# RWKV attention and a gated feed-forward on one core: channel loads of the filled rows only

## The chip, the core and the metric

The kernel runs on one core of a Trainium2 chip. The metric is the device time of one execution in microseconds (us). One core has a TensorE (PE, matmuls; its weight loads are shown as PEld), a VectorE (DVE), a ScalarE (ACT), a GpSimd (POOL), a SyncE (SP) that issues nearly all of this kernel's transfers, and 16 DMA engines that carry them out.

## What is computed

A linear attention with a decaying state (4 batches, 8 heads, 768 tokens, 48 channels per head) feeds a gated feed-forward with 3072 tokens, width 384 and inner width 1536. Cut to what matters:

```python
for t in range(S):
    kt, vt, rt = k[:, :, t], v[:, :, t], r[:, :, t]
    cur = einsum('bhd,bhe->bhde', u[None] * kt, vt)
    y[:, :, t] = einsum('bhd,bhde->bhe', rt, state + cur)
    state = w[None, :, :, None] * state + einsum('bhd,bhe->bhde', kt, vt)
x = y.transpose(0, 2, 1, 3).reshape(B * S, H * D)
out = (sigmoid(x @ w_gate) * (x @ w_val)) @ w_out
```

## The kernel before

The attention is worked off in chunks of 64 tokens (12 of them), each split into two groups of heads: 24 groups, numbered n. A group's r and k come by channels in a tile `chan` (128 partitions x 2 x 512 floats, 4 KB per partition) and its k and v by tokens in a tile `toks`. A head has 48 channels, and two heads lie in one tile, so partitions 0 to 47 and 64 to 111 of `chan` hold data and partitions 48 to 63 and 112 to 127 hold zeros, which the host wrote into the input. `load_channels` (line 97) takes a buffer out of a pool of three and loads all 128 rows with one transfer of 512 KB (line 100).

A `chan` tile is read by `bonus_keys` (ACT, L273, the first eight groups), `queries` (L294, on POOL or DVE), `keys` (DVE, L300, which multiplies the k half in place) and `scores` (PE, L341), which reads the rows 0 to 47 and 64 to 111 alone. `apply` (PE, L313) makes the attention output, `x_high` and `x_low` (L449, L453) write it into the tile `xt` of the feed-forward, and `fills` moves the channels of one pair of heads to their rows inside `xt` with small transfers of 16 rows (`fill`, L457). The feed-forward of a tile of two chunks is twelve slices f: `up` (PE, L495) reads `xt`, and `down` (PE, L533) sums into three accumulators. Its weights come as 64-bit words, are loaded once in the first part (`load_weights`, L223) and turned into two parts by DVE, ACT and POOL.

The order on every engine is the program's order. The first eight groups and the first tile are written out by hand in a string `START`; in it `L.n` is `load_channels(n)`, `X.n` `load_tokens(n)`, `W.f` `load_weights(f)`, `F.n` `fills(n)`. Its channel loads come in the order 0, 1, 2, 3, 4, 7, 5, 6. A loop over slices then does the other sixteen groups and loads each of them about two groups ahead. SP issues its transfers in this order as well. Its transfers use eight semaphores in turn (DMAHW0 to DMAHW7 in the listings below), and each transfer waits until the one eight places before it has landed, so no more than eight are under way.

Of the kernel before, what the change touches and what calls it, by code (L numbers as in the profile page):

```python
# [9 lines left out]
F32 = mybir.dt.float32  # L10
# [7 lines left out]
B, H, S, D = 4, 8, 768, 48  # L18
DM, DF = H * D, 1536
P = 128  # L20
# [37 lines left out]
def rwkv_then_moe(ctx: ExitStack, tc: tile.TileContext, wd, ch, tk, rt, ut, wt, rk0, vn0, wd0, out):  # L58
    nc = tc.nc
# [7 lines left out]
    ring = ctx.enter_context(tc.tile_pool(name="ring", bufs=3, space=PSUM))  # L67
    pacc = ctx.enter_context(tc.tile_pool(name="pacc", bufs=1, space=PSUM))
    main = ctx.enter_context(ExitStack())
    ach = main.enter_context(tc.tile_pool(name="ach", bufs=3))  # L70
    atk = main.enter_context(tc.tile_pool(name="atk", bufs=3))
    adk = main.enter_context(tc.tile_pool(name="adk", bufs=2))
    xp = main.enter_context(tc.tile_pool(name="xp", bufs=2))
# [2 lines left out]
    def two_banks():  # L76
        return ps.tile([P, 2, 512], F32, name="sc")
# [14 lines left out]
    nc.sync.dma_start(out=wu, in_=wd)  # L92
    w = wu[:, 0]

    chan, toks = {}, {}

    def load_channels(n):
        c, g = GROUPS[n]
        chan[n] = ach.tile([P, 2, 512], F32, name="chan")
        nc.sync.dma_start(out=chan[n], in_=ch[c, g])  # L100

    def load_tokens(n):
        c, g = GROUPS[n]
# [229 lines left out]
    def scores(n):  # L333
        t, r, k = dec[n], chan[n][:, 0], chan[n][:, 1]
        sc = ga[n] = two_banks()
        for kk, rr, at in ((k, t[:, 0], 0), (t[:, 1], r, 256))[: 1 if n >= FIRST else 2]:
            for p, p2 in PP:
                o = at + (2 * p + p2) * C
                for be, gm in QUARTERS:
                    row, cs = slice(64 * be, 64 * be + D), (4 * p + 2 * (be ^ gm) + p2) * C  # L340
                    nc.tensor.matmul(  # L341
                        sc[64 * gm : 64 * gm + 64, be ^ gm, o : o + C],
                        kk[row, cs : cs + C], rr[row, cs : cs + C], start=True, stop=True,
                    )

    def keep(n):
        sc, t = ga.pop(n), score[n % 2]
        if n >= FIRST:
            nc.vector.copy_predicated(
                t.rearrange("q (m i) -> q m i", m=8),  # L350
                masks[:, 1].bitcast(I32).unsqueeze(1).broadcast_to([P, 8, C]),
                gains[n % 2].unsqueeze(2).broadcast_to([P, 8, C]),
            )
        for m, at in ((0, 0), (1, 256))[: 1 if n >= FIRST else 2]:
            nc.vector.copy_predicated(  # L355
                t.rearrange("q (b m i) -> q b m i", b=2, m=4),
                masks[:, m].bitcast(I32).unsqueeze(1).unsqueeze(1).broadcast_to([P, 2, 4, C]),
                sc[:, :, at : at + 256].rearrange("q b (m i) -> q b m i", m=4),
            )

    def apply(n):
        c, g = GROUPS[n]
        v, t = toks[n][:, 1], score[n % 2]
        yb[n] = one_bank(), one_bank()
        if c:
            from_state(n)
            if n < FIRST or n + 1 == len(GROUPS):
                nc.tensor.drain()
            else:
                scores(n + 1)  # L370
                if GROUPS[n][0] < NC - 1:
                    outer(n, ga[n + 1][:, :, 256:512])
                for b in range(2):
                    nc.vector.tensor_copy(seen[:, b : b + 1], yb[n][b][0:112, 0:1])
        for p, p2 in PP:
            for s in range(2):
                for gm in range(2):
                    be, row = gm ^ s, slice(64 * gm, 64 * gm + 64)
                    m, at = D if s else 64, (4 * p + 2 * s + p2) * D
                    i = (4 * s + 2 * p + p2) * C  # L380
                    into_y(
                        n, s, be, m, slice((2 * p + p2) * C, (2 * p + p2 + 1) * C),
                        v[row, at : at + m], t[row, i : i + C], True,
                    )
# [203 lines left out]
    def finish(i):  # L588
# [8 lines left out]

    steps = {
        "L": load_channels, "X": load_tokens, "W": load_weights, "A": bonus_keys, "R": queries,
        "k": keys, "T": token_keys, "Z": scores, "K": keep, "I": apply, "O": outer,  # L600
        "d": decay_state, "s": add_state, "h": x_high, "l": x_low, "F": fills, "D": finish,
        "tc": constants, "tk": channel_table, "ti": inverses, "tp": token_powers,
# [15 lines left out]
    for step in START.split():  # L618
        name, _, arg = step.partition(".")
# [12 lines left out]
    def load(n):  # L632
        load_channels(n)
        load_tokens(n)

    n = FIRST
# [5 lines left out]
    for i in range(n0, len(items)):  # L642
        ti, h, f = items[i]
# [4 lines left out]
        if i == n0 + 2:  # L648
            gain(n)
            scores(n)  # L650
            keep(n)
            load(n + 2)
# [35 lines left out]
    with tc.If(bad != 0):  # L688
        with ExitStack() as g:
# [22 lines left out]
            with tc.For_i(0, NC) as c:  # L712
                for p in range(NP):
                    nc.sync.dma_start(
                        out=rkc[:, p].rearrange("q a b i -> q (a b i)"),
                        in_=rk0[bass.ds(c, 1), p].rearrange("o q x -> (o q) x"),
                    )
                with tc.For_i(0, C) as i:
                    for lo, side in ((0, 1), (64, 0)):
# [3 lines left out]
                        for p in range(NP):  # L723
                            nc.sync.dma_start(
                                out=vb[lo : lo + D, p], in_=src[:, p].broadcast_to([D, B, 64])
# [25 lines left out]
                    out=xg[bass.ds(c, 1)].rearrange("o q p t -> (o q) p t"),  # L751
                    in_=yc.rearrange("q p b i -> q p (b i)"),
# [3 lines left out]
            with tc.For_i(0, NC, 2) as c:  # L756
                for j in range(3):
                    for to, lo, n, p in (
# [3 lines left out]
                            out=xr[to : to + n, j],  # L762
                            in_=xg[bass.ds(c, 2), lo : lo + n, p].rearrange("c q t -> q c t"),
# [108 lines left out]
```

## Time and profile before

| | us |
|---|---|
| median of 3 runs | 541.75 (540.87 to 541.93) |
| profiled execution | 540.73 |
| its span | 538.94 |
| PE busy in the span | 518.4 (96%) |
| DVE busy | 216.4 (40%) |
| DMA traffic of SP's queue | 46.81 MB, 25.4% of the span of 16 engines |
| `chan` loads | 24 of 512 KB, median 4.9 from issue to landing |

The profiled execution is read by stretches: the share of busy time over the whole span hides that PE waits only in the first 110 us, where the transfers are dense too. "Landing" is the moment at which the last of a transfer's 16 engines has reported; a row of the transfers in a window gives the time from the start of the issue to it.

### The profile page before, as it was taken

How to read it: one execution, taken by the hardware profiler on the slowest of the kernel's cores; microseconds unless marked ns; L12 is line 12 of the kernel's file. 1: busy time of each engine (PE TensorE's matmuls, PEld its weight loads, DVE VectorE, ACT ScalarE, POOL GpSimd, SP SyncE). 2: the span in 40 equal slices, each digit the busy share in tenths (PEclk: the TensorE clock that was granted, in tenths of full speed). 3: DMA queues.
4: the chain of work that ended last, by engine and by line, in shares of the span. 5: the costliest groups of instructions: out<-in, count | busy, mean ns of one | idle time of the engine just before them, and what ended most of it. 6: DMA issues, size and time to landing. Idle time of an engine off the chain costs nothing.

```text
span 538.9 us, 12058 instructions
## 1 busy us (share of the span) xinstructions
PE 518.4 (96%) x5268; PEld 425.6 (79%) x5268; DVE 216.4 (40%) x375; ACT 171.3 (32%) x354; POOL 174.8 (32%) x159
## 2 busy tenths in 40 slices
PE   2889999999999999999999999999999999999996
PEld 2778878788788887888888888888888887888885
DVE  7999989912343342432413414313414311111111
ACT  5485755522132322231332222312322212221121
POOL 3424022122814444244145144143242311111120
PEclk9999999999999999999999999999999999999998
DMA  8895705053022214220303402203400001100001
GB/s 318 312 338 217 286 1 186 15 205 128 2 86 86 66 50 144 85 74 12 95 3 103 145 5 82 65 30 106 144 1 16 11 2 19 60 1 1 0 1 63
DMA packets 15706, 48.03 MB, mean 89 GB/s; under 512 B 2368, under 2 KB 5056, under 8 KB 14240
## 3 DMA queue, kind: packets, MB, share of 16 engines
q1 hardware_dynamic: 15360, 46.81, 25.4%
q8 instruction: 43, 0.70, 0.5%
q10 hardware_dynamic: 288, 0.39, 0.2%
q14 instruction: 15, 0.12, 0.1%
HBM read 40.12 MB, written 4.72 MB: 83 GB/s over the span
## 4 chain that ended last, share of the span: by engine, by line
PE 91%; DMA 4%; DVE 1%; SPq 1%; issue 1%; ACT 0%; POOL 0%; DVEq 0%; ACTq 0%; POOLq 0%
PE ring L495 56%; PE acc L533 27%; PE ring L313 5%; PE sc L341 2%; DMA xt<-xt 1%; DMA chan<-in_ch 1%; PE sc L396 1%; DMA wr<-in_wt 1%; SPq L457 1%; PE sc L533 1%; POOL dec L294 0%; DVE wf L236 0%; DVE wx L246 0%; ACT wx L243 0%; ACT wf L229 0%
## 5 line engine op out<-in xcount | busy, mean ns | idle before, releaser
L495 PE MATMUL ring<-xt,wx 128*128 128x512 f32 (+1 forms) x1332 | 316.4, 391 | 1.4 <-DMA xt<-xt 1.2
L495 PEld LDWEIGHTS ring<-xt,wx 128*128 128x128 f32 x1332 | 246.1, 190 | 56.6 <-issue 1.3
L517 POOL TENSOR_TENSOR h<-sg,h 128x512 fp32r<-128x512 f32 (+1 forms) x68 | 86.7, 1276 | 298.8 <-ACT h L513 298.8
L533 PE MATMUL acc<-h,wx 128*128 128x512 f32 (+1 forms) x666 | 161.1, 383 | 0.0
L508 DVE TENSOR_TENSOR sg<-ring,sg 128x512 f32<-128x512 f32 (+1 forms) x74 | 49.9, 676 | 275.6 <-PE ring L495 275.6
L533 PEld LDWEIGHTS acc<-h,wx 128*128 128x128 f32 x666 | 119.6, 188 | 24.4
L504 ACT ACTIVATE sg<-ring 128x512 f32<-128x512 f32 (+1 forms) x74 | 43.4, 587 | 184.3 <-PE ring L495 181.2
L513 ACT CAST h<-sg 128x512 fp32r<-128x512 f32 (+1 forms) x74 | 45.3, 613 | 112.0 <-DVE sg L508 111.1
L415 ACT ACTIVATE state<-state,every 112x96 f32<-112x96 f32 x80 | 23.5, 365 | 26.2 <-PE ring L313 26.2
L294 POOL TENSOR_TENSOR dec<-chan,every 128x512 f32<-128x512 f32 x21 | 25.9, 1233 | 17.0 <-DMA chan<-in_ch 12.7
L453 DVE TENSOR_TENSOR xt<-ring,xt 112x256 fp32r<-112x256 f32 (+1 forms) x52 | 20.0, 419 | 24.9 <-ACT xt L449 24.4
L341 PE MATMUL sc<-dec,chan 48*64 48x64 f32 x768 | 17.4, 231 | 7.9 <-DVE dec L294 7.9
L355 DVE COPY_PREDICATED score<-masks,sc 128x512 f32<-128x512 int32 x32 | 23.9, 745 | 1.5 <-PE sc L341 0.6
L449 ACT CAST xt<-ring 112x256 fp32r<-112x256 f32 (+1 forms) x52 | 17.1, 373 | 19.6 <-PE ring L313 17.0
L341 PEld LDWEIGHTS sc<-dec,chan 48*64 48x64 f32 x768 | 15.0, 145 | 9.3 <-DVE dec L294 7.9
L313 PE MATMUL ring<-score,toks 64*48 64x64 f32 (+1 forms) x768 | 18.7, 230 | 3.7 <-POOL dec L294 1.6
L304 POOL TENSOR_TENSOR toks<-toks,tabn 128x384 f32<-128x384 f32 x20 | 21.1, 1059 | 1.7 <-ACT tabn L194 1.6
L313 PEld LDWEIGHTS ring<-score,toks 64*48 64x48 f32 (+1 forms) x768 | 15.3, 133 | 5.1 <-POOL dec L294 1.8
L313 PEld LDWEIGHTS ring<-dec,state 48*48 48x48 f32 (+1 forms) x704 | 12.4, 127 | 8.3 <-issue 7.4
L300 DVE TENSOR_TENSOR chan<-chan,every 128x512 f32<-128x512 f32 x24 | 17.2, 715 | 0.9 <-ACT dec L273 0.9
L246 POOL TENSOR_TENSOR wx<-wf,wx 128x1152 fp32r<-128x1152 f32 (+1 forms) x3 | 6.8, 2262 | 31.9 <-ACT wx L243 31.9
L282 POOL TENSOR_TENSOR dec<-dec,toks 128x384 f32<-128x384 f32 x16 | 16.3, 1017 | 1.2
(61 smaller groups left out, 260.0 us busy)
## 6 DMA issues: line engine op xcount, KB each, us to landing
wr<-in_wt SPq DMA_DIRECT2D x11, 1152.0 KB, 8.0
chan<-in_ch SPq DMA_DIRECT2D x24, 512.0 KB, 4.9
toks<-in_tk SPq DMA_DIRECT2D x24, 400.0 KB, 5.0
out_y<-wf SPq DMA_DIRECT2D x16, 256.0 KB, 2.3
dec<-in_rt SPq DMA_DIRECT2D x16, 192.0 KB, 2.6
xt<-xt SPq DMA_DIRECT2D x30, 64.0 KB, 2.3
wr<-in_wt SPq DMA_DIRECT2D x2, 576.0 KB, 5.4
xt<-xt SPq DMA_DIRECT2D x12, 32.0 KB, 5.1
```

The lines of the kernel that those rows point to most:

```text
L294: eng.tensor_tensor(v4(t[:, 0]), v4(chan[n][:, 0]), bc2(table_of(n)), ALU.mult)
L304: eng.tensor_tensor(v4(k), v4(k), bc2(tabn[:, 4 * g : 4 * g + 4]), ALU.mult)
L313: nc.tensor.matmul(yb[n][bank][64 * half : 64 * half + m, cs], lhsT, rhs, start=first, stop=stop, skip_group_check=True,)
L341: nc.tensor.matmul(sc[64 * gm : 64 * gm + 64, be ^ gm, o : o + C], kk[row, cs : cs + C], rr[row, cs : cs + C], start=True, stop=True,)
L355: nc.vector.copy_predicated(t.rearrange("q (b m i) -> q b m i", b=2, m=4), masks[:, m].bitcast(I32).unsqueeze(1).unsqueeze(1).broadcast_to ...
L415: nc.scalar.activation(st[:, p, s], st[:, p, s], AF.Copy, scale=pw[0:112, 4 * g + 2 * p + s, 64:65],)
L495: nc.tensor.matmul(o[:, self.cols], w[a][:, g * DM + kt * P : g * DM + (kt + 1) * P], self.x[:, kt, b, self.cols], start=(k == 0), stop=(k ...
L504: nc.scalar.activation(sg[:, c], self.pair[f][0][:, c], AF.Sigmoid)
L508: nc.vector.tensor_tensor(sg[:, c], self.pair.pop(f)[1][:, c], sg[:, c], ALU.mult)
L513: nc.scalar.copy(out=h[:, 0, c], in_=sg[:, c])
L517: eng.tensor_tensor(h[:, 1, c], self.sg.pop(f)[:, c], h[:, 0, c], ALU.subtract)
L533: nc.tensor.matmul(acc[:, to], w[a][:, 2 * DM + d * P : 2 * DM + (d + 1) * P], h[:, b, cols], start=(f == 0 and k == 0 and self.cols.start ...
```

## The change

`chan` is no longer a rotating pool of three buffers but three named tiles, held in a list. The first load into each still takes all 128 rows. Every later load (21 of 24) is two transfers of 48 rows, 192 KB each; the zero rows stay from the first load (`keys` multiplies them in place, and zero stays zero). A buffer goes back to the list when the `scores` of its group have been written down in the program.

```diff
-    ach = main.enter_context(tc.tile_pool(name="ach", bufs=3))
+    ach = main.enter_context(tc.tile_pool(name="ach", bufs=1))
...
+    CHANNELS = slice(0, D), slice(64, 64 + D)
     chan, toks = {}, {}
+    cbuf = [ach.tile([P, 2, 512], F32, name=f"chan{i}") for i in range(3)]
 
     def load_channels(n):
         c, g = GROUPS[n]
-        chan[n] = ach.tile([P, 2, 512], F32, name="chan")
-        nc.sync.dma_start(out=chan[n], in_=ch[c, g])
+        whole = len(chan) < 3
+        chan[n] = cbuf.pop(0)
+        for rows in (slice(0, P),) if whole else CHANNELS:
+            nc.sync.dma_start(out=chan[n][rows], in_=ch[c, g, rows])
...
     # at the end of scores(n)
+        cbuf.append(chan[n])
```

On SP, before, from the weights of slice 2 on (`wr`): two channel loads (groups 7 and 5) stand ahead of the six small fills of `xt` for group 2.

```order
L223 DMA wr<-in_wt 128x1152 [waits DMAHW3_49]
L105 DMA toks<-in_tk 128x800 [waits DMAHW4_49,PE_49,Pool_49]
L223 DMA wr<-in_wt 128x1152 [waits DMAHW5_49]
L223 DMA wr<-in_wt 128x1152 [waits DMAHW6_49]
L105 DMA toks<-in_tk 128x800 [waits DMAHW7_49,PE_49,Pool_49]
L100 DMA chan<-in_ch 128x1024 [waits DMAHW0_49]
L100 DMA chan<-in_ch 128x1024 [waits DVE_49,DMAHW1_49,PE_49,Activation_49]
L457 DMA xt<-xt 16x2x256 [waits DMAHW2_49,DVE_49]
L457 DMA xt<-xt 16x2x256 [waits DMAHW3_49]
L457 DMA xt<-xt 16x2x256 [waits DMAHW4_49]
L457 DMA xt<-xt 16x2x256 [waits DMAHW5_49]
L457 DMA xt<-xt 16x2x256 [waits DMAHW6_49]
```

The sixth fill of this batch (not in the piece) waits on DMAHW7, which the `toks` load shown in the fifth row uses. On SP in the same place now, from that `toks` load on:

```order
L109 DMA toks<-in_tk 128x800 [waits DMAHW1_49,PE_49,Pool_49]
L104 DMA chan_97<-in_ch 48x1024 [waits DMAHW2_49]
L104 DMA chan_97<-in_ch 48x1024 [waits DMAHW3_49]
L104 DMA chan_95<-in_ch 48x1024 [waits DVE_49,DMAHW4_49,PE_49,Activation_49]
L104 DMA chan_95<-in_ch 48x1024 [waits DMAHW5_49,PE_49]
L462 DMA xt<-xt 16x2x256 [waits DMAHW6_49,DVE_49]
L462 DMA xt<-xt 16x2x256 [waits DMAHW7_49]
L462 DMA xt<-xt 16x2x256 [waits DMAHW0_49]
L462 DMA xt<-xt 16x2x256 [waits DMAHW1_49]
L462 DMA xt<-xt 16x2x256 [waits DMAHW2_49]
L462 DMA xt<-xt 16x2x256 [waits DMAHW3_49]
```

Two issues more stand ahead of the fills, and the semaphores have moved: the last three fills wait for the `toks` load and for the two halves of group 7's load, where before they waited for the two `wr` loads and the `toks` load.

On PE, in the loop, the first sixteen products of one `scores`; before:

```order
L341 MATMUL sc<-dec,chan 64x64 [waits DMAHW5_49,Pool_49]
L341 MATMUL sc<-dec,chan 64x64 x15
```

and now:

```order
L345 MATMUL sc<-dec,chan_97 64x64 [waits DMAHW7_49,Pool_49]
L345 MATMUL sc<-dec,chan_97 64x64
L345 MATMUL sc<-dec,chan_97 64x64 [waits DMAHW0_49]
L345 MATMUL sc<-dec,chan_97 64x64 x13
```

The third product, the first that reads the rows 64 to 111, has a wait of its own for the second half. DVE's `keys` and POOL's `queries` now wait for two transfers in one place.

## Rows read from the trace of the kernel before

**Rows 1.** The page: busy time, share of the span, instructions of each engine.
```profile
PE 518.4 (96%) x5268; PEld 425.6 (79%) x5268; DVE 216.4 (40%) x375; ACT 171.3 (32%) x354; POOL 174.8 (32%) x159
```

**Rows 2.** Stretches: us, length, PE, PEld, DVE, ACT, POOL busy (instructions), clock, DMA share, GB/s.
```profile
31.00:39.00 8.00, 6.39 (x184) 5.51 (x182) 7.86 (x14) 5.76 (x16) 1.94 (x3) 1.00 0.88 320
39.00:50.00 11.00, 10.21 (x212) 9.49 (x213) 10.83 (x17) 6.09 (x16) 6.72 (x7) 1.00 0.52 183
50.00:110.00 60.00, 59.38 (x643) 47.68 (x642) 54.53 (x67) 35.68 (x59) 9.97 (x6) 1.00 0.38 136
110.00:430.00 320.00, 320.00 (x3160) 260.17 (x3159) 100.62 (x209) 84.13 (x186) 125.27 (x109) 1.00 0.22 72
```

**Rows 3.** The chain that ended last, 29 to 45 us: start, us, what.
```profile
31.56 0.09 SPq L457
31.65 0.04 issue
31.69 7.41 DMA xt<-xt
39.10 0.14 issue
39.24 2.53 PE ring L495 x18
```

**Rows 4.** Instructions by time on PE: start, us, what [idle before <- releaser].
```profile
22.01 1.08 PE L313 MATMUL ring<-toks 64*64 64x48 f32 x30 [0.38 <-DVE xt L453]
...
23.02 4.21 PE L495 MATMUL ring<-xt,wx 128*128 128x256 f32 x18
...
39.24 2.53 PE L495 MATMUL ring<-xt,wx 128*128 128x256 f32 x18 [1.18 <-DMA xt<-xt]
```

**Rows 5.** SP's issues by time, 3 to 36 us: start, us, what.
```profile
3.09 1.22 SPq L100 DMA_DIRECT2D chan<-in_ch  x2
4.36 0.98 SPq L105 DMA_DIRECT2D toks<-in_tk  x2
9.98 0.33 SPq L100 DMA_DIRECT2D chan<-in_ch  x1
...
15.28 0.33 SPq L100 DMA_DIRECT2D chan<-in_ch  x1
16.16 0.33 SPq L105 DMA_DIRECT2D toks<-in_tk  x1
16.54 4.59 SPq L457 DMA_DIRECT2D xt<-xt  x6
21.17 0.58 SPq L223 DMA_DIRECT2D wr<-in_wt  x1
...
29.32 0.33 SPq L105 DMA_DIRECT2D toks<-in_tk  x1
29.70 0.92 SPq L100 DMA_DIRECT2D chan<-in_ch  x2
31.05 4.95 SPq L457 DMA_DIRECT2D xt<-xt  x6
...
34.59 1.42 SPq L457 DMA_DIRECT2D xt<-xt  x2
```

**Rows 6.** Transfers in windows that hold one issue: count, KB, us to landing.
```profile
chan<-in_ch SPq DMA_DIRECT2D x1, 512.0 KB, 7.2
...
chan<-in_ch SPq DMA_DIRECT2D x1, 512.0 KB, 7.7
...
toks<-in_tk SPq DMA_DIRECT2D x1, 400.0 KB, 8.8
...
chan<-in_ch SPq DMA_DIRECT2D x1, 512.0 KB, 6.4
...
chan<-in_ch SPq DMA_DIRECT2D x1, 512.0 KB, 5.5
...
xt<-xt SPq DMA_DIRECT2D x1, 32.0 KB, 2.5
...
toks<-in_tk SPq DMA_DIRECT2D x1, 400.0 KB, 6.1
...
chan<-in_ch SPq DMA_DIRECT2D x1, 512.0 KB, 8.4
...
xt<-xt SPq DMA_DIRECT2D x1, 32.0 KB, 4.5
```

**Rows 7.** Stretches, columns as in rows 2: whole loads; last landings; fills alone.
```profile
5.00:13.00 8.00, 3.47 (x120) 3.31 (x124) 6.82 (x12) 5.33 (x15) 1.46 (x1) 1.00 1.02 412
19.40:22.90 3.50, 1.82 (x51) 1.51 (x44) 3.38 (x8) 2.21 (x4) 2.14 (x2) 1.00 0.52 110
...
82.47:82.97 0.50, 0.50 (x4) 0.41 (x3) 0.50 (x2) 0.43 (x2) 0.00 (x0) 1.00 0.76 123
```

**Rows 8.** DMA queues from 13.0 to 14.3 us: packets, MB, share of 16 engines.
```profile
q8 instruction: 1, 0.02, 5.3%
```

**Rows 9.** Waits of the whole run: engine, line <- releaser: us, times, longest us.
```profile
POOL dec L294 <- DMA chan<-in_ch: 12.7, 3, 6.1
...
ACT dec L273 <- DMA chan<-in_ch: 7.7, 4, 3.0
```

## Prediction

> **What bounds the kernel now.** I read the page first, then the stretches, then the chain, and only then the transfers. PE is busy 96% of the span [rows 1]; its idle time is 538.9 - 518.4 = 20.5 us. The stretches say where that lies: none from 110 to 430 us, 0.62 us from 50 to 110, 0.79 us from 39 to 50, 1.61 us from 31 to 39 [rows 2], and most of the rest before. So a transfer matters only where PE still waits, in the first 40 us. One such wait is for transfers by name: the chain goes from SP's second batch of fills (L457) through 7.41 us of transfer to PE's `up` at 39.24 [rows 3], which stood idle for 1.18 us because of it [rows 4]. Those fills stand behind the loads of groups 7 and 5, which the change makes smaller. The channel loads themselves are waited for three times on POOL and four times on ACT, the longest being 6.1 us [rows 9]; both engines have that time to spare in the first part, and none of these waits is PE's.
>
> The sums are made against the profiled execution, 540.73 us, and carried over to the median, 541.75, by adding 1.0.
>
> **Fewer bytes.** 21 loads drop 32 rows of 4096 bytes: 131,072 bytes each, 2.75 MB of 46.81 in all. In the dense stretch the engines move 412 GB/s [rows 7], so one load is worth 0.32 us of queue. Two whole loads, issued at 3.09 and 3.85, land at 3.1 + 7.2 = 10.3 and 3.9 + 7.7 = 11.6 [rows 5, 6]: 1.3 us for 512 KB, where 412 GB/s would give 1.27. The fixed part of a transfer in the queue is thus some 0.03 us, and the second transfer costs that much again. I take 0.27 us gained per load if narrow transfers run as fast as wide ones. Sixteen of the 21 loads belong to the loop, where the DMA share is 0.22 and PE has no idle time [rows 2]: worth nothing. Of the five in the first part, groups 3 and 4 go out before the first fills (9.98 and 15.28), groups 7 and 5 just before the second (29.70), and group 6 after them [rows 5]. Only the pair 7 and 5 stands in front of something that PE waits for: at most 2 x 0.27 = 0.54 us off the 1.18 us.
>
> **Narrower rows.** No row of the trace shows a load from memory onto 48 partitions, so I bound it. The wide loads give 412 / (1.02 x 16) = 25.2 GB/s per busy engine; the fills, 16 rows of 4 KB, at 82.5 us and alone in the queue, give 123 / (0.76 x 16) = 10.1 [rows 7]. Half a load has three rows, 12,288 bytes, on each of 16 engines: 0.49 us at the one rate, 1.22 us at the other, so a pair takes 0.97 to 2.43 us where a whole load takes 1.3: from -0.3 to +1.1 us a load. 48 rows are nearer to 16 than to 128, and I take +1.0 for the engines that run together. The fills read SBUF too, so their low rate may be owed to the reading; that is the chance of the fast end.
>
> **Who sets the landing.** A landing is that of the slowest of 16 engines. The `toks` load asked for at 4.9 lands at 4.9 + 8.8 = 13.7, and group 3's channels behind it at 10.0 + 6.4 = 16.4 [rows 5, 6]: 2.7 us for a transfer that took 1.3 before. In between one engine carried an instruction packet, 5.3% of 16 engines for 1.3 us, that is 1.1 us on one engine [rows 8]. From 19.40 to 22.90, while the loads and fills end, the engines are busy 0.52 of the time [rows 7]: most are done and a few are late. The same at the second batch: `toks` at 29.3 + 6.1 = 35.4, group 7 at 29.7 + 7.2 = 36.9 (the row of the 3.1 issue reads the same), group 5 at 30.3 + 8.4 = 38.7, so 3.3 us for two loads. The punctual engines therefore have spare time, I estimate 1.5 to 2 us (2.7 less 1.3 already at group 3). Two pairs at +1.0 put them about where the late ones were, while a late engine works through its rows alone, without the crowding, and is early by up to 2 x 0.27. Fills at 39.24: between -0.5 and +0.5 us, I take +0.1. The first fills have the same cover, and PE is at other work until 22.01 + 1.08 = 23.1 when it begins on them at 23.02 [rows 4]: 0.
>
> **More issues.** 21 more on SP, 0.33 to 0.46 us each [rows 5]. In the loop SP mostly waits for compute. Before the first fills, group 4's second half fits between 15.28 + 0.33 and the `toks` issue at 16.16 [rows 5]. Before the second batch two more issues move the first fill from 31.05 to about 31.8, but it lies in the queue behind group 5's landing at 38.7 in any case: 0. Without that cover it would be 0.75 us.
>
> **The semaphores in turn.** This speaks against the change. The last two fills of the second batch now wait for both halves of group 7's load, 36.9 us, where before they were asked for at 34.6 and, the last, at 35.4 [rows 5]. A fill asked for late takes 2.5 us (the one of 20.5 [rows 6]), so the last one lands at 36.9 + 2.5 = 39.4, and the last of before at 35.4 + 4.5 = 39.9 [rows 6]: 0. Only if the halves land beyond 37.4 does it cost, and it holds just the seventh of PE's 18 products, due 6/18 of 2.53 us, or 0.8 us, after the first [rows 4]; I bound it at +0.4. In the first batch the weights of slice 2, at 21.17, now wait for group 4's second half, which before was whole at 15.3 + 5.5 = 20.8 [rows 5, 6]: 0 to +0.3.
>
> **More waits on compute.** PE meets a second wait in some 20 `scores`, DVE and POOL in their two steps likewise. In the loop no wait for a `chan` load shows, all three of POOL's lying in the first part [rows 9], and PE stays at 320.00 of 320 us [rows 2] with a wait of this kind at the head of every `scores`: 0.
>
> **Sum.** 540.73 + 0.1 = 540.8; as a median **541.8 us**, no change.
>
> **Rivals.** *Slow narrow rows reach PE.* If all engines slow alike, the late ones too, the two pairs ahead of each batch cost 2 x 1.1 = 2.2 us. The first fills then hold PE at 23.02, where the cover is some 0.8 us: +1.4. The second hold it at 39.24: +2.2 more. PE idles 0.79 + 0.62 = 1.4 us later on [rows 2], mostly for DVE, and can win that back: +2.2 in all, 543.9. It decides from the point where two pairs outgrow the punctual engines' spare time. For it: the fills' 10.1 GB/s. Against it: landings that one late engine sets. The Trainium skill speaks for it: "SBUF — State Buffer", section "Door 1: The DMA port swizzle", says that a transfer's rate goes by how many of 16 ports its partitions reach, that 0 to 63 reach only eight, and gives 196 GB/s for them against 328 for all at 1 MiB; by that a half would take an estimated 1.0 us. The trace agrees in kind: the fills are slower per engine than the wide loads.
>
> *The bytes reach PE.* If narrow rows run at the wide rate, the second fills land 0.54 us sooner, and group 5's POOL step with them: 541.2, and 540.6 if all of the 1.18 us goes. Against it: DVE is busy 10.83 of the next 11 us and 54.53 of the next 60 [rows 2], so that PE may meet DVE later instead.
>
> *It moves no fewer bytes to any effect.* The queue drains as before because the late engine is late for its instruction packet, not for its rows: 541.7, inside the forecast.
>
> **How the numbers follow.** A measurement of this kernel tells about 0.2%, 1.1 us, from no change. Forecast (541.2 to 542.8, with the semaphores' +0.4 and the last rival in it): 0.66. Slow rows reaching PE in full: 0.17; in part, 542.8 to 543.2: 0.06. Bytes reaching PE: 0.11, of which 0.06 end more than 1.1 us below the median of before. A hundredth of the forecast falls out on either side. So faster 0.07, same 0.69, slower 0.24. The range from 540.9 to 543.4 leaves out about 0.06 below and 0.13 above.
>
> **What would show it.** SP's queue falls from 46.81 to 44.06 MB. PE begins its `up` between 38.7 and 39.8 us, and the wait for the fills stays its only wait for a transfer. A pair lands about 2 us after what stood before it, alone in the loop 1 us later than now. From 110 us on PE stays without idle time. I am wrong if PE's `up` at 23.02 or at 39.24 moves by more than 0.8 us, if the stretch from 39 to 110 us gains or loses idle time beyond that, or if the loop shows waits for `chan`.

## The result, and the profile after

The changed kernel takes 545.58 us (544.80 to 547.61, 5 runs), the kernel before 541.72 us (540.87 to 541.93, 5 runs): a ratio of 1.0075, 95% interval 1.0056 to 1.0094. It is 3.9 us slower, where no change was forecast; a second comparison, on another chip, gave 1.0047 (1.0025 to 1.0069). Lines of the changed kernel stand four or five further down: fills 462, `up` 500, `down` 538, channel loads 104.

The page (lines of busy time and of SP's queue: packets, MB, share of 16 engines). The bytes fell as the change says, 46.81 to 44.06 MB, but the engines' share *rose*, from 25.4% to 26.8%:

```profile
PE 520.0 (96%) x5268; PEld 427.3 (79%) x5268; DVE 216.6 (40%) x375; ACT 171.2 (31%) x354; POOL 174.6 (32%) x159
...
q1 hardware_dynamic: 15024, 44.06, 26.8%
```

The stretches of [rows 2] and, first, one inside the second batch of loads (us, length, busy time of PE, PEld, DVE, ACT, POOL, clock, DMA share, GB/s):

```profile
34.60:37.20 2.60, 2.03 (x82) 1.70 (x73) 2.53 (x3) 1.54 (x6) 0.00 (x0) 1.00 1.05 176
...
31.00:39.00 8.00, 6.91 (x191) 6.14 (x187) 7.87 (x14) 6.05 (x16) 1.89 (x2) 1.00 1.00 275
39.00:50.00 11.00, 8.78 (x149) 8.46 (x141) 8.51 (x13) 3.90 (x10) 4.26 (x4) 0.84 0.61 202
50.00:110.00 60.00, 59.21 (x704) 47.76 (x701) 55.55 (x70) 37.43 (x64) 12.41 (x8) 1.00 0.35 131
110.00:430.00 320.00, 320.00 (x3146) 260.11 (x3148) 100.43 (x207) 83.57 (x184) 124.24 (x108) 1.00 0.25 67
```

The same 2.6 us in the kernel before:

```profile
34.60:37.20 2.60, 2.57 (x88) 2.24 (x84) 2.57 (x3) 1.90 (x6) 0.00 (x0) 1.00 0.89 324
```

All engines are busy there, most of them on half loads, and they move 176 GB/s where whole loads ran at 324. A half of 196,608 bytes thus takes about 1.1 us and a pair 2.2, against 1.3 for a whole load.

The chain of the changed kernel (start, us, what; for [rows 3]), and PE by time (for [rows 4]):

```profile
32.92 8.26 DMA xt<-xt
41.19 0.14 issue
41.32 3.92 PE ring L500 x18
```

```profile
23.55 4.18 PE L500 MATMUL ring<-xt,wx 128*128 128x256 f32 x18 [0.32 <-DMA xt<-xt]
...
41.32 3.92 PE L500 MATMUL ring<-xt,wx 128*128 128x256 f32 x18 [2.22 <-DMA xt<-xt]
```

PE's third start (its `up` on the second batch) is at 41.32 instead of 39.24, idle for 2.22 us ahead of it instead of 1.18. Two profiles more of each kernel, taken later, make the table below. PE's last group of matmuls (the row `sc<-h,wx ... x3` at the end of PE's time line) gives PE's end; what lies from its start to the end of the span is the tail.

| | third start | last PE group | span | tail |
|---|---|---|---|---|
| before, 3 profiles | 39.24, 39.26, 38.96 | 533.43, 533.50, 533.16 | 538.9, 540.3, 538.8 | 5.5, 6.8, 5.6 |
| changed, 3 profiles | 41.32, 40.73, 41.35 | 536.24, 535.92, 536.51 | 543.8, 543.2, 543.0 | 7.6, 7.3, 6.5 |

On average PE ends 2.9 us later (536.22 against 533.36), the tail is 1.1 us longer (7.1 against 6.0), and the span 4.0 us longer. The time went to two places, then, and only the first is one that the prediction looked at.

Single profiles scatter, and here they do so to one side. The three profiled executions of the kernel before took 540.73, 542.19 and 540.73 us where the medians beside them were 541.75, 542.69 and 541.72; those of the changed kernel that have a median beside them lie at it (545.58) or 0.2 above (545.01 and 544.80). A difference of PE ends from the 533.36 can thus be too large by up to 1.0 us, and where profiles and times disagree below, the times decide.

### The profile page after: what moved, and what is told of

It reads as the page before. It is cut to its first block, busy times and chain, and to the rows that moved or that the text cites. A ratio compares the mean times of both kernels' runs of the same rounds, so it can differ in the third digit from the quotient of the medians.

```text
span 543.8 us, 12116 instructions
## 1 busy us (share of the span) xinstructions
PE 520.0 (96%) x5268; PEld 427.3 (79%) x5268; DVE 216.6 (40%) x375; ACT 171.2 (31%) x354; POOL 174.6 (32%) x159
## 3 DMA queue, kind: packets, MB, share of 16 engines
q1 hardware_dynamic: 15024, 44.06, 26.8%
## 4 chain that ended last, share of the span: by engine, by line
PE 90%; DMA 5%; DVE 1%; issue 1%; SPq 1%; ACT 0%; POOL 0%; ACTq 0%; POOLq 0%; DVEq 0%
PE ring L500 55%; PE acc L538 26%; PE ring L317 5%; DMA chan<-in_ch 2%; PE sc L345 2%; DMA xt<-xt 2%; PE sc L401 1%; DMA wr<-in_wt 1%; PE sc L538 1%; POOL dec L298 0%; DVE wf L240 0%; DVE wx L250 0%; ACT wx L247 0%; SPq L227 0%; DVE wf L239 0%
## 5 line engine op out<-in xcount | busy, mean ns | idle before, releaser
L420 ACT ACTIVATE state<-state,every 112x96 f32<-112x96 f32 x80 | 23.4, 363 | 26.2 <-PE ring L317 26.2
```

The source lines that it names most:

```text
L420: nc.scalar.activation(st[:, p, s], st[:, p, s], AF.Copy, scale=pw[0:112, 4 * g + 2 * p + s, 64:65],)
```

## Experiments

The theory after the result: 48 rows use the engines badly, so a pair holds the queue 0.9 us longer than a whole load, and this reaches PE at its third start. Rivals: the 21 more transfers and semaphores as such; the waits of the fills; scatter.

**Transfers alone.** A kernel with loads from the same array and nothing else (no attention, no feed-forward), back to back in groups of one shape: whole tiles; rows 0 to 47 only; rows 0 to 47 and 64 to 111 in turn; 64, 32, 16 and 112 rows; column halves on all 128 rows; the halves on two queues.

```python
def both_halves():
    for _ in range(8):
        load(LO)      # rows 0 to 47
        load(HI)      # rows 64 to 111
```

> Transfers alone: the kernel computes nothing and writes zeros; it loads the channel input over and over, in groups of one shape that fill the queue, between groups of whole loads (128 rows of 4 KB). If few partitions slow a transfer: rows 0 to 47 again and again, and rows 0 to 47 in turn with 64 to 111, move 160 to 200 GB/s (1.0 to 1.2 us a half), halves of 64 rows 200 to 220, 32 rows 190 to 220, 16 rows about 105, 112 rows in one transfer 350 to 370, and two column halves of 128 rows the 410 of whole loads; low and high halves asked for on two queues at once come back to 300 or more. If only bytes and a fixed part of some 0.03 us count: every group from 32 rows up moves 370 to 410 GB/s, and a half of 48 rows takes 0.5 us.

Stretches inside the groups, in the order just named (us, length, busy time of POOL, clock, DMA share, GB/s):

```profile
5.00:18.00 13.00, 0.00 (x0) 1.00 1.03 408
25.00:37.00 12.00, 0.00 (x0) 1.00 1.04 156
57.00:67.00 10.00, 0.00 (x0) 1.00 1.03 216
90.00:101.00 11.00, 0.00 (x0) 1.00 1.03 246
...
180.00:193.00 13.00, 0.00 (x0) 1.00 1.03 275
213.00:220.00 7.00, 0.00 (x0) 1.00 1.05 387
240.00:252.00 12.00, 0.00 (x0) 1.00 1.04 201
```

The share is full in all of these (32 and 16 rows, left out here, didn't fill the queue), so the rate is that of the shape. A pair of halves takes 2 x 196,608 bytes / 216 GB/s = 1.82 us, a whole load 524,288 / 408 = 1.28: fewer bytes, more time. The expectation was too slow for the pair (0.91 us a half, not 1.0 to 1.2) and for 64 rows (246, not 200 to 220), a little too fast for rows 0 to 47 alone (156, not 160 to 200), and wrong for 112 rows (275, not 350 or more) and for two queues (201, not 300 or more). Column halves, the same number of transfers on all rows, run at 387.

**The number of transfers.** The changed kernel with each later load as two transfers of all 128 rows, half of the columns each: as many issues, semaphores and waits, but wide rows.

```diff
-        for rows in (slice(0, P),) if whole else CHANNELS:
-            nc.sync.dma_start(out=chan[n][rows], in_=ch[c, g, rows])
+        for cols in (slice(0, 2),) if whole else (slice(0, 1), slice(1, 2)):
+            nc.sync.dma_start(out=chan[n][:, cols], in_=ch[c, g, :, cols])
```

> The changed kernel with the same number of transfers in the same places, but each second transfer is one of the two column halves of all 128 rows (2 KB per row), so all bytes are loaded and no transfer is narrow. If narrow rows delayed PE: the up at 41.3 in the changed kernel begins at 39.2 to 39.7 again and nothing of the 2.8 us on PE is left. If the number of transfers or the turn of the semaphores did it: it stays at 41 or later. For the tail (from the end of the last compute instruction to the end of the span, 3.9 us before, 6.0 us in the changed kernel): if the longer program of SP is its cause, it stays at about 6.0 and the median is 543.5 to 544.2; if not, 3.9 and 541.5 to 542.0.

1.001 (0.9996 to 1.0023): no difference. PE by time at the third start:

```profile
38.76 2.61 PE L500 MATMUL ring<-xt,wx 128*128 128x256 f32 x18 [0.97 <-DVE xt L458]
```

Earlier than in the kernel before. PE's delay is owed to the narrow rows, not to the count. Its last PE group starts at 532.88 and its span is 539.8, so the tail is 6.9 us, as long as in the changed kernel.

**Which loads.** Only the 16 loads of the loop split (`whole = n < FIRST`), and only the five of the first part (`whole = len(chan) < 3 or n >= FIRST`).

> Only the 16 loads of the loop are split into 48-row halves; the eight of the first part are whole. Narrow rows or turn of semaphores in the first part as the cause of PE's delay: PE's up begins at 39.2 as before, no shift on PE anywhere. Tail by the length of SP's program (16 issues and their waits more): about 6.0 us and a median of 543.4 to 544.0; tail by anything of the first part: 3.9 us and 541.5 to 542.

> Only the five loads of groups 3 to 7 in the first part are split, the 16 of the loop are whole. PE's delay as in the changed kernel: up at 41.0 to 41.6, PE 2.5 to 3.0 us late from there to the end. Tail: by the length of SP's program it depends on where its code ends, with 5 issues more nearer to before, 3.9 us, and a median of 544.2 to 544.8; if any late PE lengthens the tail, 6.0 us and 546.

Loop only: 1.0006 (0.9990 to 1.0022). First part only: 1.0052 (1.0036 to 1.0068). PE's third start in the one and in the other:

```profile
39.18 2.53 PE L500 MATMUL ring<-xt,wx 128*128 128x256 f32 x18 [1.59 <-DVE state L431]
```

```profile
41.46 2.40 PE L500 MATMUL ring<-xt,wx 128*128 128x256 f32 x18
```

Five loads carry it; by the time the loop hides its sixteen, as forecast. PE's last group starts at 535.28 with the five, 1.9 us late instead of the 2.5 to 3.0 expected, and at 534.23 with the loop alone, 0.9 us late where no shift was expected: as late as in the kernels with tiny transfers below, and within what single profiles scatter. Of the five, next, all but groups 7 and 5 split (`whole = len(chan) < 3 or n in (5, 7)`), and groups 7 and 5 alone (`whole = n not in (5, 7)`):

> The changed kernel, but the channel loads of groups 7 and 5, the two that stand just ahead of the fills of the second expert's columns, go as one transfer of 128 rows; the other split loads stay split, and what is computed is the reference's. Theory: the pairs of these two loads (2.1 us each instead of 1.28 in the profile of the changed kernel) are what makes TensorE's third start late; then TensorE takes up the second expert's columns at 39.3 to 39.8 us (changed kernel 41.32, before 39.24), its clock does not fall, and the end on TensorE is 0 to 0.8 us later than before, the run 0.5 to 2 us longer than before, most of that behind the last computation. Rival: the earlier pairs (groups 3, 4 and 6) already set the delay, which the queue only hands on; then TensorE takes it up at 40.5 us or later and the run stays 2.5 us or more longer than before.

> The kernel before, but the channel loads of groups 7 and 5 alone, the two just ahead of the fills of the second expert's columns, go as two transfers of 48 rows. Theory: a pair takes 2.1 us in the queue where a whole load takes 1.28, so two pairs bring the fills, and with them TensorE's third start, 1.6 us later: 40.5 to 41.2 us instead of 39.24 (the changed kernel 41.32), the end on TensorE 1 to 2 us later, the run 1 to 2.5 us longer. Rival: groups 3, 4 and 6 cost as much in the changed kernel, and these two alone are hidden by the waits of the fills on the buffers: then TensorE's third start stays below 39.8 us and the run within 0.7 us of before.

PE at the third start, with 7 and 5 whole, then with 7 and 5 alone split:

```profile
39.63 0.47 PE L500 MATMUL ring<-xt,wx 128*128 128x256 f32 x2 [0.15 <-ACT h L518]
40.75 2.16 PE L500 MATMUL ring<-xt,wx 128*128 128x256 f32 x16 [0.65 <-DVE xt L458]
```

```profile
39.93 0.60 PE L500 MATMUL ring<-xt,wx 128*128 128x256 f32 x3 [1.65 <-DVE score L360]
40.93 3.36 PE L500 MATMUL ring<-xt,wx 128*128 128x256 f32 x15 [0.40 <-DMA xt<-xt]
```

PE's last group starts at 534.39 in the first and at 535.50 in the second, 1.0 and 2.1 us after the kernel before's 533.36. As times: 1.0029 (1.0012 to 1.0047) and 1.0015 (0.9999 to 1.0030), which is 1.6 and 0.8 us; for the second, 1 to 2.5 were expected. So by PE's end in one profile each, the two loads just ahead of the second batch of fills cost more than the rest, and by the times rather less. How the cost is divided among the five loads stays open.

There are two ways by which it reaches PE. With 7 and 5 whole, the sixteen products at 40.75 wait for DVE and not for a fill. This comes from groups 3 and 4: the weights of slice 2 stand behind group 4's load in the queue, and ACT, whose order is fixed, waits for them before it rounds the weights of slice 1, which DVE and then PE's second `up` need. ACT and PE in the kernel before, then in the third profile of the changed kernel:

```profile
26.54 1.32 ACT L229 ACTIVATE wf<-wr 128x1152 f32<-128x1152 f32 x1 [0.81 <-DMA wr<-in_wt]
...
30.35 2.39 PE L495 MATMUL ring<-xt,wx 128*128 128x256 f32 x18 [0.19 <-DVE wx L246]
```

```profile
28.73 1.29 ACT L233 ACTIVATE wf<-wr 128x1152 f32<-128x1152 f32 x1 [2.57 <-DMA wr<-in_wt]
...
32.50 2.40 PE L500 MATMUL ring<-xt,wx 128*128 128x256 f32 x18 [1.68 <-DVE wx L250]
```

These weights land at 26.4, 26.2 and 26.0 us in the three profiles of the kernel before, and at 26.9, 28.1 and 28.6 in those of the changed one. The second `up` starts between 30.00 and 30.99 us in all eleven profiles in which groups 3 and 4 are loaded with all their rows, and between 30.95 and 32.86 in the six in which they are split. In the second profile of the changed kernel it is this way that sets the third start:

```profile
40.73 0.98 PE L500 MATMUL ring<-xt,wx 128*128 128x256 f32 x6 [1.25 <-DVE xt L458]
```

The kernel with 7 and 5 alone split shows how the delay by the other way, the fills, comes about. Transfers by single issues (count, KB, us from issue to landing), the last weights ahead of the second batch (slice 7, issued at about 24 us) and the `toks` load behind them, in the kernel before, with 7 and 5 split, and in the changed kernel:

```profile
wr<-in_wt SPq DMA_DIRECT2D x1, 1152.0 KB, 10.5
...
toks<-in_tk SPq DMA_DIRECT2D x1, 400.0 KB, 6.1
```

```profile
wr<-in_wt SPq DMA_DIRECT2D x1, 1152.0 KB, 10.5
...
toks<-in_tk SPq DMA_DIRECT2D x1, 400.0 KB, 7.6
```

```profile
wr<-in_wt SPq DMA_DIRECT2D x1, 1152.0 KB, 12.1
...
toks<-in_tk SPq DMA_DIRECT2D x1, 400.0 KB, 8.4
```

With 7 and 5 split, the weights land as before, and the `toks` load behind them, whole and ahead of every half in the queue, takes 1.5 us longer. It is no scatter: this load lands at 36.1 us or earlier in all eleven profiles with both of the loads behind it on all rows, and at 36.9 or later in the six with one or both split. Its landing is that of the slowest engine. The trace holds the report of each of the 16 engines, of which the views print the last alone: in the kernel before, twelve have reported this load by 34.2 us and the other four from 34.8 to 35.4; with 7 and 5 split, twelve by 34.1 and the other four from 35.5 to 36.9. So the punctual engines go on to the halves as early as ever, and it is the late ones, still on whole rows, that take longer. That they are slowed by what the others carry is the reading that fits; no row shows what it is that they share.

**A load moved behind the fills.** If the queue ahead of the fills sets the third start, a load fewer there helps the kernel before too. Group 7's load goes behind the six fills; the same then in the changed kernel.

```diff
-T.2 O.2 h.2 l.2 X.4 s.2 H.0 Z.3 K.3 A.4 q.0 k.4 R.4 c.4 j.2 U.1 g.1 I.3 O.3 L.7 L.5 m.1 d.3 h.3 H.1
-l.3 A.5 D.0 w.2 R.5 Z.4 T.4 s.3 K.4 F.2 U.2 k.5 g.2 m.2 q.1 D.1 H.2 U.3 g.3 Z.5 j.4 m.3 X.5 I.4 O.4
+T.2 O.2 h.2 l.2 X.4 s.2 H.0 Z.3 K.3 A.4 q.0 k.4 R.4 c.4 j.2 U.1 g.1 I.3 O.3 L.5 m.1 d.3 h.3 H.1
+l.3 A.5 D.0 w.2 R.5 Z.4 T.4 s.3 K.4 F.2 L.7 U.2 k.5 g.2 m.2 q.1 D.1 H.2 U.3 g.3 Z.5 j.4 m.3 X.5 I.4 O.4
```

> The kernel before, with whole loads, but the channel load of group 7 is issued after the six fills of the second expert's columns instead of ahead of them; nothing else. Theory: at the third start TensorE waits for the queue's transfers in their turn, so one transfer of 1.28 us fewer ahead of the fills brings TensorE's start from 39.24 to 38.0 to 38.5 us, and the run gets 0.5 to 1.2 us shorter (540.5 to 541.2 where before stands at 541.7). Rival: the wait that is shortened is taken over by the projection's conversion or by the next fills, and the run is within 0.5 us of before; if the channels of group 7 then come late to the first engine that needs them, the run is up to 2 us longer.

> The kernel before with the channel load of group 7 behind the six fills, once more on another chip. Theory: TensorE's third start 0.8 to 1.5 us earlier than in the kernel before, the run 0.4 to 1 us shorter. Rival: the first comparison's 0.7 us was scatter; then the run is within 0.3 us of before.

> The changed kernel, split loads and all, with the channel load of group 7 issued after the six fills as well. Theory: what costs is the 0.8 us that a pair takes longer than a whole load, per pair ahead of the fills; with one pair (2.1 us) fewer there TensorE starts the second expert's columns at 39.2 to 39.7 us instead of 41.32, and the run lies 1.5 to 2.5 us over before, of which 1.5 to 2 us lie behind the last computation. Rival: the number of waits and issues on the queue costs, wherever they stand: then the start is at 40.5 us or later and the run 3 us or more over before.

In the kernel before: 0.9987 (0.9974 to 1.0000), and on another chip 0.9988 (0.9973 to 1.0003). PE at the third start, first profile:

```profile
37.95 0.50 PE L495 MATMUL ring<-xt,wx 128*128 128x256 f32 x2
38.78 2.17 PE L495 MATMUL ring<-xt,wx 128*128 128x256 f32 x16 [0.33 <-DVE xt L453]
```

PE starts 1.3 us earlier (1.7 in the second profile) but waits for DVE next, so that sixteen of the 18 products start only 0.4 us earlier (38.78 and 38.83), and its last group starts at 532.89 and 532.91, 0.5 us before the kernel before's. Both comparisons say 0.7 us faster than before, and each interval alone reaches 1: likely the best of these kernels, not a proven one. The changed kernel gains less than expected: 1.0050 (1.0032 to 1.0069), a third start at 40.81 and PE's last group at 535.74. In that profile PE is late already at its second `up` (32.86 where before has 30.35), by the way of groups 3 and 4; this part was left out of the expectation.

**Scatter and the tail.** The two kernels again, and the kernel before with tiny transfers on SP's queue: 4 bytes each into a tile that nobody reads, 21 of them (twice) and 48.

```diff
+    spare = const.tile([1, 2], F32, name="spare")
...
         nc.sync.dma_start(out=toks[n], in_=tk[c, g])
+        for i in range((n >= 8) + (8 <= n < 13)):
+            nc.sync.dma_start(out=spare[0:1, i : i + 1], in_=wd[0:1, 0, 0:1])
```

The expectations count from the last instruction of ScalarE, 1.3 to 2 us behind the start of PE's last group; by that count the kernel before's three tails are 3.9, 4.6 and 4.1 us, the changed kernel's 6.0, 5.7 and 4.5. The last is a miss: 5.3 to 6.2 was expected, and 4 to 5 was the sign of scatter. The clock in the second profile of the changed kernel is another: it was expected to fall and held.

> The kernel before, with 21 more transfers issued on SyncE's queue, of 4 bytes each into a tile that nobody reads, behind the token loads of the groups from 8 on (as many issues as the change adds in all); the loads are whole. Theory: the end of the run behind the last computation grows because SyncE's program is longer or ends elsewhere in its store, whatever the transfers carry: the span ends 5 to 6 us after the last computation instead of 3.9, TensorE's order of time is within 0.3 us of before, and the run is 1 to 2 us longer (542.7 to 543.7 where before stands at 541.7). Rival: the tail follows from something else in the changed kernel (late transfers, the clock, the buffers); then the tail stays at 3.9 us and the run within 0.5 us of before.

> The kernel before once more, for a second profile: how far TensorE's third start (39.24 us in the first profile), the time between the last computation and the end of the span (3.9 us) and SyncE's waits behind its last branch (2.3 us in all) differ from one execution to another. Theory: within 0.8 us each. Rival: they differ by as much as the changed kernel's do (2 us each), and then neither is an effect of the change.

> The changed kernel once more, for a second profile and beside the others on one chip. Theory: TensorE's third start at 40.6 to 42 us, idle for over 1 us ahead of it and the granted clock down for some us behind that; 5 to 6.3 us from the last computation to the end; the run 2.5 to 4.5 us longer than before. Rival: the fall of the clock and the long end belong to the one execution profiled; then the start is late but the clock holds, the end takes 4 us, and the run is 1 to 2 us longer.

> The kernel before, a third profile. Theory (more issues on SyncE lengthen the end): 3.8 to 4.8 us from the last computation to the end of the span. Rival (scatter): anything from 3.8 to 6.

> The kernel before with 21 transfers of 4 bytes more on SyncE's queue, a second profile. Theory: 5 to 6 us from the last computation to the end of the span, as in its first profile (5.4). Rival (scatter): as in the kernel before, 3.8 to 4.8 us.

> The kernel before with 48 transfers of 4 bytes more on SyncE's queue, three behind each token load from group 8 on. Theory: the end is longer than the kernel before's by at least as much as with 21 (5 us or more from the last computation to the end of the span), the run 1 to 3 us longer than before. Rival (scatter): 3.8 to 4.8 us and a run within 0.5 us of before. If the place of SyncE's last code in its store decides, and not the count, the end may also be as short as before's.

> The changed kernel, a third profile. Theory: 5.3 to 6.2 us from the last computation to the end of the span; TensorE's end 2.3 to 3 us later than in the kernel before. Rival (scatter): an end of 4 to 5 us.

| | third start | last PE group | span | tail |
|---|---|---|---|---|
| 21 tiny, 21 tiny, 48 tiny | 40.08, 39.60, 39.63 | 534.26, 534.64, 534.20 | 541.5, 541.7, 541.2 | 7.2, 7.1, 7.0 |

Times: 1.0028 (1.0015 to 1.0042) with 21, 1.0022 (1.0011 to 1.0033) with 48. From ScalarE's last instruction the tail is 5.4 us in all three. So a longer program on SP, with whole loads, is slower, by 1.5 and 1.2 us, and comes out with the changed kernel's mean tail; 48 cost no more than 21. How much of it is scatter is less sure than three profiles look: the kernel with group 7 moved, as long on SP as the kernel before, has 6.3 and 7.3 in its two (spans 539.2 and 540.2). With those, five profiles of the short program average 6.3, and ten of the programs with 16 or more issues added (7.6, 7.3, 6.5, 7.2, 7.1, 7.0, and 6.9, 6.8, 6.4, 7.0 of the column halves, the loop alone, 7 and 5 whole, and the changed kernel with group 7 moved) 7.0: a lengthening of 0.7 to 1.1 us. SP's waits behind its last branch (line: us, times, longest), in the kernel before, the changed one, and with 21 tiny transfers:

```profile
SPq L688 <- SPq L688: 2.3, 3, 1.1
```

```profile
SPq L693 <- SPq L693: 4.1, 1, 4.1
```

```profile
SPq L691 <- SPq L691: 3.4, 1, 3.4
```

SP stands once for 3.4 to 4.1 us right behind the branch at the program's end, where it waits for nothing that the profile names but itself; in the kernel before it stands three times for 1.1 at most (4.0 in all in the second profile, the longest 2.2, and 2.3 again in the third). But this doesn't part the long programs from the short ones: with group 7 moved, as long on SP as before, it is 3.5 in all in both profiles, and 3.4 and 3.5 with the column halves and with the loop alone. What SP does in that time isn't shown. That its code has to be fetched there is a guess.

PE's end is 1.0 us later in these three too, not within the 0.3 us that were expected, though up to 49 us SP issues exactly what it issued before; at 39 to 48 us a delay of 0.4 to 1.1 us is there already. The column halves, with as many issues, don't have it. A part of this is the choice of execution: the profiles of the kernel before and of the column halves lie 0.5 to 1.0 and 0.7 us below their medians, those with tiny transfers only 0.1 where a median is known. The rest is not explained.

## Why the prediction was wrong, point by point

**What bounds the kernel: right for the loop.** In the changed kernel, with all its loads split, PE is at 320.00 of 320 us, no wait for `chan` shows there, and splitting the loop alone gives no difference in time. The first 40 us hold most of the loss, but not all: there is the tail, and 0.7 to 1.0 us between the third start and PE's end.

**Fewer bytes and narrower rows: right as a sum.** The term of +1.0 us a load stands against 2.2 - 1.3 = +0.9 in the second batch and +0.5 among transfers alone. The bytes that were to give 0.27 us back are in both numbers. The Trainium skill has a reason that fits in "SBUF — State Buffer", section "Door 1: The DMA port swizzle (why `[64,N]` ≈ `[32,N]`)": partitions 0 to 63 reach eight of 16 ports; the trace agrees, with 156 GB/s for rows 0 to 47 alone against 408 for all. The 275 GB/s of rows 0 to 111, which lie on both sides of row 63, are not explained by that. The Trainium skill's page "DMA: Bandwidth & Descriptors", section "Rules for kernel authors", advises one transfer of 128 partitions in place of two on disjoint halves, since the two serialize; the trace agrees, 1.82 us for the pair against 1.28.

**Who sets the landing: this step failed.** It held that one late engine works through its rows alone, without the crowding, so that the punctual ones have 1.5 to 2 us to spare; the sum at the third start was +0.1, and it was +2.1, +1.5 and +2.1 in three profiles. At this start the sign named for being wrong came, a move of more than 0.8. The spare time was there, and the halves used it up and more: twelve engines report the first fill of the second batch from 36.7 to 37.6 us in the kernel before and from 38.9 to 40.0 in the first profile of the changed one; the last reported at 38.9 before. That alone would be up to 1.1 us. The rest is what was said of the late engine: there are four in these two profiles, and while the others carry halves they are slowed too. The `toks` load ahead of every half lost 1.5 us with 7 and 5 split; in the changed kernel it lands 3.0 us later than before, and the first fill, when the late engines have caught up a little, 2.1, at 41.0. So nothing covered the pairs. The term for the weights of slice 2, 0 to +0.3, was too small as well: they land 0.7, 1.9 and 2.4 us after the mean of the kernel before. In the two later ones fifteen engines have reported by 26.9 us and one is 1.2 and 1.7 us behind, and why that one is isn't shown. The prediction followed these weights no further, though ACT's wait for them leads to PE's second `up`.

**The rival that happened.** "Slow narrow rows reach PE" had 0.17. It gave +1.4 at 23.02, +2.2 at 39.24, and 1.4 won back: +2.2 in all. The profiles give +0.5 (23.55), +2.1, and nothing won back: +2.9 at PE's end. The time to be filled was put down to DVE, and DVE is late itself. From 23 to 50 us it is busy for 24.0, 25.4 and 23.4 us in the three profiles of the changed kernel, against 26.5, 26.4 and 26.4 in those of the kernel before; in the second, DVE is busy 10.82 of the 11 us from 39 to 50, as before, while PE idles 2.67 of them; in the first it also waits 1.71 us for PE, at PE's low clock. From its third start to its last group PE needs 494.9, 495.2 and 495.2 us, against 494.2 in all three of the kernel before. So the delay grew behind the third start, where the rival had it shrink. That the rival's sum came nearest to the time is in part luck: its first term was too large, its last had the wrong sign, and the tail is in none.

**The semaphores in turn.** The condition named there came true: the halves of group 7 land at about 30.33 + 9.1 = 39.4 us, beyond 37.4, and the last fills are asked for only then. What it costs beside the late first fill can't be told apart in these runs; in the second profile of the changed kernel one short wait for a fill, 0.19 us, follows behind the start.

**More issues: half right.** On the queue they cost nothing, as the column halves show. At the end of the program they may cost 0.7 to 1.1 us of tail, which no term of the sum contained; the trace of before couldn't show it.

**The clock.** In the changed kernel's first profile the granted clock fell right after the 2.22 us of idle PE (us, length, busy times, clock, DMA share, GB/s):

```profile
41.80:45.20 3.40, 3.40 (x17) 3.40 (x17) 1.47 (x1) 1.77 (x4) 3.40 (x4) 0.50 0.94 351
45.20:47.00 1.80, 1.80 (x17) 1.80 (x16) 1.62 (x3) 0.41 (x1) 0.00 (x0) 1.00 1.06 363
```

For 3.4 us PE ran at the lower of its two levels, 1.2 GHz, and seventeen products took 3.40 us where the next seventeen took 1.80. It isn't the cause of the delay: the second profile has no fall (1.00 from 39 to 50 us) and ends on PE at 535.92, 2.6 us late, against 2.9 and 3.2 where it fell. At PE's end no price of the fall shows: from the third start to PE's last group it is 495.2 us without it and 494.9 and 495.2 with it.

## What to carry to other kernels

Price a transfer by the measured rate of its shape, not by its bytes: in a full queue, leaving out a quarter of the rows by splitting made the load 0.5 to 0.9 us slower. If a landing is set by a few late DMA engines, don't count the others' spare time as cover: what they carry in it can slow the late ones too. And follow each delayed transfer through the engine that waits for it to the next engine, even if the wait at hand isn't on the engine that bounds the kernel. A load just ahead of a transfer that PE waits for did better moved behind it (0.7 us, twice, but not proven) than made smaller by a split.

## What the runs showed of the hardware that was not expected

One transfer of rows 0 to 111 runs at 275 GB/s, 1.67 us for 458,752 bytes: slower than all 128 rows, 1.28 us for more bytes. So in a full queue leaving out the last 16 rows alone would cost as well. Halves of 64 rows, which leave no byte out, reach 246 GB/s against 408 as one transfer, and a second queue for the other half doesn't raise the rate (201 against 216 on one).

SP's program length may have a price at the very end: with 16 to 48 more issues the span ends 0.7 to 1.1 us later behind PE's last group on average, whatever the transfers carry. The profiles of one kernel scatter by as much (5.5 to 6.8 us in the kernel before), so this is a likely effect and not a shown one.

The granted clock can fall after an idle stretch of 1.4 us (third profile of the changed kernel, where PE then runs at 1.2 GHz for 3.4 us; 0.84 on average from 39 to 50 us) and stay up after one of 1.63 us (21 tiny transfers, 1.00 there), so the length of the wait alone doesn't tell.
